# Two residual layers on one core: where SBUF tiles lie, and at which steps a fused unit prepares its second half

## The chip, the cores and the metric

The program runs on one core of a Trainium2 chip. The metric is the device time of an execution in microseconds; lower is better. A program is executed several times for its median, and once more under the hardware profiler.

## The reference

Two layers alternate, twice each, on 2048 tokens of 1024 features, all in float32 (B_* and A_* are weights):

```
x = A_q
x = x + A(layernorm(x))      # q * (long causal convolution of shifted k times v)
x = x + B(layernorm(x))      # relu(x @ w1 + b1)**2 @ w2 + b2
x = x + A(layernorm(x))
x = x + B(layernorm(x))
```

w1 is 1024 x 3584 and w2 is 3584 x 1024. The convolution runs along the tokens, per feature; its result does not depend on x, which only multiplies it.

## The kernel before

**Tiling.** Tokens are worked in four blocks of 512. Seven units are done in the order of `ORDER`; each is the dense layer B of one block (`(layer, block)`), and the convolution's products, its transforms and the layer norms are woven between its steps. A step is twelve matmuls. Every float32 operand is split into a rounded part and a rest ("hi" and "lo", type fp32r), so that one product takes three matmuls: hi by hi, hi by lo, lo by hi (`mm3`, L348 to L351). The weights' rounded part is cast on ScalarE (L1072), the rest subtracted on VectorE or GpSimd (L1080; the table `WLO` names the engines in turn, V or G, for a phase of the program). Some split weights are kept in HBM and come back as pairs (whl<-wd_m).

**Two kinds of step.** In a step of the first matrix (called m1) activations move through the array and weights stand in it: moving operand `xh` or `xl`, standing operand `whl`. In a step of the second matrix the weights move and the squared activations stand: moving `whl`, standing `rh` or `rl`, and in unit 5 also tiles named cx, cg, cp and fy (called w2 here).

**Pools.** SBUF tiles come from pools that lie one behind the other: const, pre, mw, and then cv, with a pool for the first block or ml behind it. mw holds a pad `pad_m` of 128 B, xh and xl (16 KiB each), 8 raw weight rows wr (2 KiB each) and 6 split weights whl (4 KiB each). cv begins with four tiles fx that take 2080 B each; the tiles that stand in the array in w2 steps follow at whole multiples of 256 B. When the convolution is over, cv is closed and a pool pp, the arena, opens at the place where cv began: a pad `pad_q` of 128 B, five tiles tq (16 KiB each), three sr (8 KiB), two zr (6 KiB). Each pool is laid out per partition, so these sizes give how far apart two operands are.

**The joint unit.** The last entry of `ORDER` handles two blocks at once (`make_duo`), called the joint unit, with a scheme of seven products for four. It has 196 steps in three phases: 28 steps a1 (m1 type, on the first of the two blocks), 70 steps b1 (moving tq, standing whl; five products for each of 14 pairs p), 98 steps c2 (moving whl, standing tq; seven products, each over the 14 pairs). Work beside the steps is put off by `lag.at(d, ...)`: it is written into the engines' queues d ticks later; there is one tick ahead of each step, then the weights' preparation (`w_advance`), then the step's matmuls. Each engine takes its own queue in order, so what is written at a tick stands behind all that was written earlier, and SyncE (SP) issues nearly all DMAs in that one order too.

While a1 runs, `side` prepares the second block's tokens for b1, 128 tokens (tt) at a time, in links k = 0 to 10: loads (0), mean and variance (1), gate and residual sum (2, `combine`), mean and variance again and a store (3), normalisation (4: scalars on VectorE, L1844, two passes on ScalarE, L1846), transposes on TensorE (5, L1853), differences (6 and 7), and the split into the five tq tiles (8 to 10). `SIDE_AT` gives for each tt the tick of its link 0; the links follow at fixed distances. PSUM results of a1 leave by ScalarE (L1886) and VectorE (L1900).

b1 leaves squared activations in HBM, in groups HD of four entries of 128 x 512 floats, in the order in which c2 uses them (`hd_put`, L1825). c2 loads a group with one DMA (`h_load`, L1968), rounds it on ScalarE (`h_hi`, L1972) and subtracts on VectorE (`h_lo`, L1977). Its buffers are the tq ring of five: at c2's opening, tiles that b1 still reads. c2 also reloads the residual rows of both blocks (`r_load`, L1993), adds the bias b2 to them on GpSimd (`r_bias`, L1996), adds the products from PSUM (`r_add`, L1999, VectorE) and stores.

Of the kernel before, what the change touches and what calls it, by code (L numbers as in the profile page):

```python
# [19 lines left out]
P = 128  # L20
# [47 lines left out]
WLO = {"b": "GGGV", "x": "GGGV", "b1": "VVG", "c2": "VG"}  # L68
SIDE_AT = ((2, 3), (3, 4), (0, 9), (1, 14))
# [177 lines left out]
def tile_h3_mlp(ctx: ExitStack, tc: tile.TileContext, q, kT, vT, shk, ssmT, ssmD, w1, b1, w2, b2,  # L247
# [61 lines left out]
    V.memset(pad_p, 0.0)  # L309
    b1t = const.tile([P, P], F32)  # L310
# [510 lines left out]
    def combine(x, y, m, r):  # L821
        for h in range(2):
            sl = slice(h * 512, (h + 1) * 512)
            V.scalar_tensor_tensor(y[:, sl], x[:, sl], m, y[:, sl], op0=OP.subtract, op1=OP.mult)
            V.scalar_tensor_tensor(x[:, sl], y[:, sl], r, x[:, sl], op0=OP.mult, op1=OP.add)

    def prep_w(l, b, lag):
# [4 lines left out]
        def early(tt, k):  # L832
# [5 lines left out]
            elif k == 1:  # L838
                combine(st["x"], st.pop("y"), mv[:, tt, 0:1], r[:, tt:tt + 1])
# [275 lines left out]
    pad_m = mw.tile([P, PAD_M], F32)  # L1115
    V.memset(pad_m, 0.0)
# [686 lines left out]
    def make_duo(xT):  # L1803
# [23 lines left out]
        def side(st, tt, k):  # L1827
            if k == 0:
                st["x"] = load_x(1, b2_, tt)
                st["s"] = arena[0].tile([P, 4, 512], F32, name="sr", bufs=3)  # L1830
                SY.dma_start(st["s"][:, 0:2].rearrange("p a n -> p (a n)"), YD[b2_][:, tt])
# [6 lines left out]
            elif k == 2:  # L1838
                r = rstd_b(st["ve"], st["sd"])
                combine(st["x"], st["s"][:, 0:2].rearrange("p a n -> p (a n)"), st["mv"][:, 0, 0:1], r)  # L1840
            elif k == 4:
                r = rstd_b(st["ve"], st["sd"])
                nr = pre.tile([P, 1], F32, name="nr", bufs=4)
                V.scalar_tensor_tensor(nr, st["mv"][:, 0, 0:1], -1.0, r, op0=OP.mult, op1=OP.mult)  # L1844
                for h in range(2):
# [119 lines left out]
        def h_load(g):  # L1965
            n = HD[g].shape[1]
            t = hs[g] = arena[0].tile([P, 2, DUO_G, 512], F32R, name="tq", bufs=5)
            SY.dma_start(t[:, 1, 0:n].bitcast(F32), HD[g])  # L1968

        def h_hi(g, i):  # L1970
            t = hs[g]
            A.copy(t[:, 0, i:i + 2], t[:, 1, i:i + 2].bitcast(F32))  # L1972

        def h_lo(g, i):
            t = hs[g]
            lo = t[:, 1, i:i + 2]
            V.tensor_sub(lo, lo.bitcast(F32), t[:, 0, i:i + 2].bitcast(F32))  # L1977
# [29 lines left out]
        def go(k, p, j, w, xT):  # L2007
# [3 lines left out]
            if k == "a1":  # L2011
                if s == 0:
                    lag.at(20, load_b2, bst)
# [6 lines left out]
            elif k == "b1":  # L2020
                if s == 0:
# [4 lines left out]
                    for x in range(n_p):  # L2026
                        lag.at(5 * x + 6, get_a11, x)
# [18 lines left out]
                for g, x in ((0, 8), (1, 5)):  # L2046
                    if left == x:
                        h_plan(g)
            else:
                if s == 0:  # L2050
                    for x, (e, h) in enumerate(((0, 1), (1, 0), (1, 1))):
                        lag.at(1 + x, r_load, e, h)
                        for n in range(4):
                            lag.at(5 + x + n, r_bias, e, h, n)
                    lag.at(8, r_load, 0, 0)
                    for n in range(4):
                        lag.at(11 + n // 2, r_bias, 0, 0, n)
                if s % DUO_G == 0 and s // DUO_G + 2 < len(HD):
                    h_plan(s // DUO_G + 2)
# [260 lines left out]
```

## Time and profile before

| | |
|---|---|
| Median of 3 runs | 2732.11 us (2728.47 to 2737.31) |
| The profiled execution, its own time | 2726.12 us |
| Span from first to last instruction | 2724.3 us |
| TensorE (PE) busy | 2661.5 us, 98% |
| VectorE (DVE) busy | 1997.0 us, 73% |
| ScalarE (ACT), GpSimd (POOL) busy | 1103.4 us, 1068.9 us |
| Mean granted TensorE clock | 0.994 |

A row of a profile view names the line of the kernel, the engine, the operation, the written tile and the tiles read (for a matmul the moving operand stands first, unless it is a transpose), how many there are, their busy time and the mean duration of one. A matmul's duration is longer than the distance to the next one, since they overlap. "Idle" is the time that an engine waited just before, with what released it. PEclk is the granted share of TensorE's clock. "SPq" is SyncE's queue, from which DMAs are issued.

### The profile page before, as it was taken

The page shows a single profiled execution, that of the slowest core. Times are in us where ns is not written, and L with a number is a line of the kernel's source. Part 1 is how long each engine was busy: PE and PEld are TensorE (multiplying, and loading weights), DVE is VectorE, ACT ScalarE, POOL GpSimd, SP SyncE. Part 2 cuts the span into 40 slices and gives each one's busy share as a digit, 9 for nine tenths or more (in the row PEclk, how much of TensorE's full clock was granted, in tenths as well). Part 3 has the DMA queues.
Part 4 walks back from the last instruction along what each step waited for, and adds up shares of the span by engine and source line. Part 5 has one row for each costly group of instructions (what it writes and reads, how often), then busy time and mean ns, then how long its engine had stood idle before and what let it go on. Part 6 is the DMA issues. An engine that isn't in the chain of part 4 may idle for free.

```text
span 2724.3 us, 36231 instructions
## 1 busy us (share of the span) xinstructions
PE 2661.5 (98%) x12433; PEld 2208.3 (81%) x12433; DVE 1997.0 (73%) x2926; ACT 1103.4 (41%) x1882; POOL 1068.9 (39%) x681
## 2 busy tenths in 40 slices
PE   7999999899999999999999999999999999999999
PEld 7888787788888888888888888888788778877887
DVE  7878888689887877779777666366777877766553
ACT  4454344334444333342333422345455454443432
POOL 2336565255542645327554365000100155536221
PEclk9999999999999999999999999999999999999999
DMA  8789898689989898788987878688898877768553
GB/s 262 260 303 312 284 308 284 219 289 371 340 290 316 309 335 293 271 305 304 334 278 259 315 271 290 214 292 285 298 313 274 292 269 236 239 237 310 203 191 122
DMA packets 379112, 761.32 MB, mean 279 GB/s; under 512 B 43936, under 2 KB 159280, under 8 KB 375856
## 3 DMA queue, kind: packets, MB, share of 16 engines
q1 hardware_dynamic: 378928, 759.01, 81.2%
q8 instruction: 98, 1.61, 0.2%
q14 instruction: 86, 0.70, 0.1%
HBM read 583.75 MB, written 175.11 MB: 279 GB/s over the span
## 4 chain that ended last, share of the span: by engine, by line
PE 81%; DMA 8%; DVE 6%; POOL 2%; SPq 1%; ACT 1%; issue 1%; DVEq 0%; ACTq 0%; POOLq 0%
PE p L350 24%; PE p L349 24%; PE p L351 24%; DMA wr<-w 2%; PE p L1156 2%; DMA whl<-wd_m 2%; PE pt L349 2%; PE pt L350 2%; PE pt L351 2%; DMA cg<-gd 1%; DMA hd<-xh 1%; DVE whl L1080 1%; DMA px<-x 0%; SPq L639 0%; DVE st L710 0%
## 5 line engine op out<-in xcount | busy, mean ns | idle before, releaser
L539 POOL TENSOR_TENSOR cp<-cx,cg 128x384 f32<-128x384 f32 (+5 forms) x288 | 544.2, 1903 | 582.0 <-DVE sm L543 387.7
L349 PE MATMUL p<-xh,whl 128*128 128x512 f32 (+1 forms) x1504 | 577.5, 384 | 2.4 <-DMA whl<-wd_m 2.4
L351 PE MATMUL p<-xh,whl 128*128 128x512 f32 (+1 forms) x1504 | 573.7, 381 | 0.6 <-POOL whl L1080 0.6
L350 PE MATMUL p<-xl,whl 128*128 128x512 f32 (+1 forms) x1504 | 573.2, 381 | 0.1
L1072 ACT CAST whl<-wr 128x512 fp32r<-128x512 f32 x545 | 331.5, 618 | 482.1 <-PE p L351 293.4
L349 PE MATMUL p<-whl,rh 128*128 128x512 f32 x1204 | 481.5, 400 | 3.1 <-ACT whl L1072 1.5
L350 PE MATMUL p<-whl,rh 128*128 128x512 f32 x1204 | 477.0, 396 | 4.5 <-DVE whl L1080 4.5
L351 PE MATMUL p<-whl,rl 128*128 128x512 f32 x1204 | 476.4, 396 | 0.0
L1080 DVE TENSOR_TENSOR whl<-wr,whl 128x512 fp32r<-128x512 f32 x479 | 426.7, 901 | 64.0 <-ACT whl L1072 59.1
L349 PEld LDWEIGHTS p<-xh,whl 128*128 128x128 f32 x1504 | 284.1, 189 | 56.8 <-issue 2.1
L351 PEld LDWEIGHTS p<-xh,whl 128*128 128x128 f32 x1504 | 283.4, 188 | 55.5 <-POOL whl L1080 0.8
L350 PEld LDWEIGHTS p<-xl,whl 128*128 128x128 f32 x1504 | 283.7, 189 | 52.6 <-DVE xl L1469 0.3
L1559 DVE TENSOR_TENSOR rl<-wr,rh 128x512 fp32r<-128x512 f32 x140 | 139.5, 997 | 183.6 <-ACT rh L1556 183.5
L350 PEld LDWEIGHTS p<-whl,rh 128*128 128x128 f32 x1204 | 227.9, 189 | 56.3 <-DVE whl L1080 6.2
L349 PEld LDWEIGHTS p<-whl,rh 128*128 128x128 f32 x1204 | 228.0, 189 | 55.8 <-DMA whl<-wd_m 3.0
L351 PEld LDWEIGHTS p<-whl,rl 128*128 128x128 f32 x1204 | 227.6, 189 | 53.2
L543 DVE TENSOR_REDUCE sm<-cp 128x128 f32<-128x384 f32 (+5 forms) x288 | 249.2, 873 | 10.1 <-POOL cp L539 10.1
L1551 ACT ACTIVATE wr<-p,b1t 128x512 f32<-128x512 f32 x138 | 95.2, 690 | 371.4 <-PE p L351 368.8
L1080 POOL TENSOR_TENSOR whl<-wr,whl 128x512 fp32r<-128x512 f32 x66 | 90.8, 1377 | 267.2 <-ACT whl L1072 264.7
L1679 DVE TENSOR_TENSOR acc<-p,acc 128x512 f32<-128x512 f32 x152 | 100.9, 686 | 87.0 <-PE p L351 86.6
L1977 DVE TENSOR_TENSOR tq<-tq 128x1024 fp32r<-128x1024 f32 x49 | 68.4, 1395 | 89.3 <-ACT tq L1972 89.3
L689 POOL TENSOR_TENSOR sm<-sm 128x512 f32<-128x512 f32 x48 | 68.8, 1433 | 132.9 <-DVE sm L543 125.5
(348 smaller groups left out, 4361.3 us busy)
## 6 DMA issues: line engine op xcount, KB each, us to landing
whl<-wd_m SPq DMA_DIRECT2D x323, 512.0 KB, 5.6
wr<-w SPq DMA_DIRECT2D x441, 256.0 KB, 5.4
wd_m<-whl SPq DMA_DIRECT2D x70, 512.0 KB, 6.4
wr<-td SPq DMA_DIRECT2D x112, 256.0 KB, 4.9
cx<-xd SPq DMA_DIRECT2D x48, 512.0 KB, 5.6
cg<-gd SPq DMA_DIRECT2D x48, 512.0 KB, 6.5
tq<-hd SPq DMA_DIRECT2D x24, 1024.0 KB, 6.9
gd<-fg SPq DMA_DIRECT2D x72, 256.0 KB, 6.3
```

Source lines behind the costliest of these rows:

```text
L349: PE.matmul(o, lh, rh, start=start, stop=False)
L350: PE.matmul(o, lh, rl, start=False, stop=False)
L351: PE.matmul(o, ll, rh, start=False, stop=stop)
L539: G.tensor_mul(pr.rearrange("p c i -> p i c"), xt[:, 0:j + 1], gt[:, j::-1])
L543: V.tensor_reduce(sm[:, ty, jj], st["pr"], axis=AX.X, op=OP.add)
L689: E.tensor_add(s[:, 1:3], s[:, 1:3], s[:, 0:1].to_broadcast([P, 2, s.shape[2]]))
L1072: A.copy(t[:, 0], raws[n]["t"])
L1080: ENG[e[n % len(e)]].tensor_sub(t[:, 1], raws[n]["t"], t[:, 0].bitcast(F32))
L1551: A.activation(r, st["o"], AF.Relu, bias=b1t[:, st["f"]:st["f"] + 1])
L1559: V.tensor_sub(st["lo"], st["r"]["t"], st["hi"].bitcast(F32))
L1679: V.tensor_add(accs[tt][:, d], o, accs[tt][:, d])
L1977: V.tensor_sub(lo, lo.bitcast(F32), t[:, 0, i:i + 2].bitcast(F32))
```

## The change

It has four parts.

**Places.** `pad_m` moves from mw into cv and becomes its first tile; `pad_q` is gone. So all of mw lies 128 B lower, cv's other tiles stay where they were, and the tq tiles lie 256 B lower than before.

**The links of `side`.** The distances from link 0 become (0, 3, 4, 5, 6, 9, 10, 11, 12, 13, 14) in place of (0, 2, 3, 4, 5, 6, 7, 8, 9, 10, 11), and some starts change. For the tile tt = 1 the convolution's part comes in two rows of the raw weights' ring, and its sr tile is taken only at link 4.

**Groups.** The first HD group has two entries in place of four, and is loaded into the two px tiles of pool pre, at the step with 12 of b1 left. The next three are loaded at the last three steps of b1; the later ones are loaded 10 steps ahead of their use (8 before) and split later after their load.

**c2's rest.** The bias is loaded at c2's fifth tick (it was in a1), the bias sums on GpSimd are spread over ticks 8 to 26 (5 to 12 before), the first product's sums on VectorE come six ticks later, and in c2 GpSimd subtracts one weight in three in place of one in two. `get_a11` comes four ticks earlier.

The diff, cut to its core:

```diff
-WLO = {"b": "GGGV", "x": "GGGV", "b1": "VVG", "c2": "VG"}
-SIDE_AT = ((2, 3), (3, 4), (0, 9), (1, 14))
+WLO = {"b": "GGGV", "x": "GGGV", "b1": "VVG", "c2": "VVG"}
+SIDE_AT = ((2, 2), (3, 4), (0, 9), (1, 11))
...
+    pad_m = cv.tile([P, PAD_M], F32)
+    V.memset(pad_m, 0.0)
...
-    pad_m = mw.tile([P, PAD_M], F32)
-    V.memset(pad_m, 0.0)
...
-        HD = [dram.tile([P, min(DUO_G, len(order) - g), 512], F32, name=f"hd{g}") for g in range(0, len(order), DUO_G)]
-        at = {x: (HD[n // DUO_G], n % DUO_G) for n, x in enumerate(order)}
+        group = [(0, n) if n < 2 else ((n - 2) // DUO_G + 1, (n - 2) % DUO_G) for n in range(len(order))]
+        HD = [dram.tile([P, DUO_G if g else 2, 512], F32, name=f"hd{g}") for g in range(group[-1][0] + 1)]
+        at = {x: (HD[group[n][0]], group[n][1]) for n, x in enumerate(order)}
...
-            pad_q = arena[0].tile([P, PAD_M], F32)
-            V.memset(pad_q, 0.0)
...
-                st["s"] = arena[0].tile([P, 4, 512], F32, name="sr", bufs=3)
-                SY.dma_start(st["s"][:, 0:2].rearrange("p a n -> p (a n)"), YD[b2_][:, tt])
+                if tt == 1:
+                    st["y"] = [row() for _ in range(2)]
+                    ys = [x["t"] for x in st["y"]]
+                else:
+                    st["s"] = arena[0].tile([P, 4, 512], F32, name="sr", bufs=3)
+                    ys = [st["s"][:, h] for h in range(2)]
+                for h, y in enumerate(ys):
+                    SY.dma_start(y, YD[b2_][:, tt, h * 512:(h + 1) * 512])
...
-            for k, d in enumerate((0, 2, 3, 4, 5, 6, 7, 8, 9, 10, 11)):
+            for k, d in enumerate((0, 3, 4, 5, 6, 9, 10, 11, 12, 13, 14)):
...
-            t = hs[g] = arena[0].tile([P, 2, DUO_G, 512], F32R, name="tq", bufs=5)
-            SY.dma_start(t[:, 1, 0:n].bitcast(F32), HD[g])
+            if g:
+                t = arena[0].tile([P, 2, DUO_G, 512], F32R, name="tq", bufs=5)
+                hs[g] = t[:, 0], t[:, 1]
+            else:
+                hs[g] = [pre.tile([P, 2, 512], F32R, name="px", bufs=2) for _ in range(2)]
+            SY.dma_start(hs[g][1].bitcast(F32), HD[g])
...
-        def h_plan(g):
+        def h_plan(g, first=4, gap=2):
             h_load(g)
             for i in range(0, HD[g].shape[1], 2):
-                lag.at(4 + i, h_hi, g, i)
-                lag.at(5 + i, h_lo, g, i)
+                lag.at(first + i // 2, h_hi, g, i)
+                lag.at(first + gap + i // 2, h_lo, g, i)
...
-                for g, x in ((0, 8), (1, 5)):
-                    if left == x:
-                        h_plan(g)
+                if left == 12:
+                    h_plan(0)
+                if left in (2, 1, 0):
+                    h_plan(3 - left, 3, 1)
...
-                    for x, (e, h) in enumerate(((0, 1), (1, 0), (1, 1))):
-                        lag.at(1 + x, r_load, e, h)
+                    lag.at(4, load_b2, bst)
+                    for x, (e, h) in enumerate(((0, 1), (1, 0), (1, 1), (0, 0))):
+                        lag.at((1, 2, 3, 15)[x], r_load, e, h)
                         for n in range(4):
-                            lag.at(5 + x + n, r_bias, e, h, n)
-                    lag.at(8, r_load, 0, 0)
-                    for n in range(4):
-                        lag.at(11 + n // 2, r_bias, 0, 0, n)
-                if s % DUO_G == 0 and s // DUO_G + 2 < len(HD):
-                    h_plan(s // DUO_G + 2)
+                            lag.at((8 + x + 3 * n, 20 + 2 * n)[x == 3], r_bias, e, h, n)
+                if (s + 10 - 2) % DUO_G == 0 and 4 <= (s + 8) // DUO_G + 1 < len(HD):
+                    h_plan((s + 8) // DUO_G + 1)
...
-                            lag.at(1 + n * (j in (1, 6, 7)), r_add, x // 2, x % 2, n, os[n])
+                            lag.at(1 + n * (j in (1, 6, 7)) + 6 * (j == 1), r_add, x // 2, x % 2, n, os[n])
```

Up to the joint unit the instructions stand in the same order on every engine as before, except for the pads' memsets. Inside it they move. The first place is ScalarE's queue in a1, from the normalisation of tt = 2 (the first sr<-px) to the first copy of its transposes (sr<-p). In the kernel before:

```order
L718 ACTIVATE sd<-mv_20309,epst 128x1
L1846 ACTIVATE sr<-px,nr,rs 128x512 x2
L718 ACTIVATE sd<-mv_20358,epst 128x1
L1895 ACTIVATE wr<-wr,b1t 128x512
L1896 ACTIVATE wr<-wr 128x512
L1886 COPY wr<-p_20335 128x512
L1846 ACTIVATE sr<-px,nr,rs 128x512 x2
L1860 COPY sr<-p_20396 128x512
```

The same piece of the changed kernel, whose lines are numbered some ten higher:

```order
L1856 ACTIVATE sr<-px,nr,rs 128x512 x2
L1905 ACTIVATE wr<-wr,b1t 128x512
L1906 ACTIVATE wr<-wr 128x512
L1896 COPY wr<-p_20325 128x512
L720 ACTIVATE sd<-mv_20379,epst 128x1
L1856 ACTIVATE sr<-px,nr,rs 128x512 x2
L1905 ACTIVATE wr<-wr,b1t 128x512
L1906 ACTIVATE wr<-wr 128x512
L1896 COPY wr<-p_20400 128x512
L1870 COPY sr<-p_20451 128x512
```

Between the normalisation of tt = 2 and the copy of its transposes there now stands the squaring and eviction work of two pairs of a1 (L1905 to L1896 twice), where that of one stood.

The second place is SyncE's queue at the end of b1. The tiles hd_20122, hd_20123 and hd_20124 are the first three groups; hd<-zr and the like are the stores of b1's results, wr<-w are c2's raw weights. Before, the first group's load stands eight steps ahead of c2, in the tq ring:

```order
L1922 DMA xl<-hd_20124 128x512
L1825 DMA hd_20142<-xl 128x512
L1968 DMA tq<-hd_20122 128x2048
L1825 DMA hd_20131<-xh 128x512
L1062 DMA wr<-w 128x512 x3
L1968 DMA tq<-hd_20123 128x2048
L1825 DMA hd_20128<-zr 128x512
```

In the changed kernel that load is gone to an earlier place (px<-hd_20122, behind the stores of the pair before), and the next groups stand here:

```order
L1932 DMA xl<-hd_20125 128x512
L1825 DMA hd_20132<-xh 128x512
L1065 DMA wr<-w 128x512
L1981 DMA tq<-hd_20123 128x2048
L1065 DMA wr<-w 128x512
L1981 DMA tq<-hd_20124 128x2048
L1065 DMA wr<-w 128x512
L1981 DMA tq<-hd_20125 128x2048
```

The loads into the tq ring moved behind the raw weights and the reloads of all pairs (xl<-hd is the reload `get_a11`), to b1's last three steps.

More of the change, by code (lines that the diff above doesn't have):

```diff
@@ L819, in prep_b, with combine @@
         return xh, xl
-    def combine(x, y, m, r):
-        for h in range(2):
+    def combine(x, ys, m, r):
+        for h, y in enumerate(ys):
             sl = slice(h * 512, (h + 1) * 512)
-            V.scalar_tensor_tensor(y[:, sl], x[:, sl], m, y[:, sl], op0=OP.subtract, op1=OP.mult)
-            V.scalar_tensor_tensor(x[:, sl], y[:, sl], r, x[:, sl], op0=OP.mult, op1=OP.add)
+            V.scalar_tensor_tensor(y, x[:, sl], m, y, op0=OP.subtract, op1=OP.mult)
+            V.scalar_tensor_tensor(x[:, sl], y, r, x[:, sl], op0=OP.mult, op1=OP.add)
     def prep_w(l, b, lag):
@@ L1829, in side @@
                 st["x"] = load_x(1, b2_, tt)
-                st["s"] = arena[0].tile([P, 4, 512], F32, name="sr", bufs=3)
-                SY.dma_start(st["s"][:, 0:2].rearrange("p a n -> p (a n)"), YD[b2_][:, tt])
+                if tt == 1:
[4 more added lines that the diff above has]
+                    ys = [st["s"][:, h] for h in range(2)]
+                for h, y in enumerate(ys):
+                    SY.dma_start(y, YD[b2_][:, tt, h * 512:(h + 1) * 512])
+                st["ys"] = ys
             elif k in (1, 3):
@@ L1844, in side @@
                 V.scalar_tensor_tensor(nr, st["mv"][:, 0, 0:1], -1.0, r, op0=OP.mult, op1=OP.mult)
+                if "s" not in st:
+                    st["s"] = arena[0].tile([P, 4, 512], F32, name="sr", bufs=3)
                 for h in range(2):
@@ L2063, in go @@
                 os = banks[0]
-                t = hs[s // DUO_G]
-                hi, lo = t[:, 0, s % DUO_G], t[:, 1, s % DUO_G]
+                hi, lo = (t[:, group[s][1]] for t in hs[group[s][0]])
                 for n in range(4):
```

20 lines of the change are left out of this document (9 added, 11 removed).

## The prediction, made before the changed kernel ran

> **What bounds the kernel now.** The page comes first. The first line of the fence is the span, the second the busy time of TensorE and its weight loads and of VectorE, then the matmul groups of the second matrix; the last two are ScalarE's and VectorE's share of preparing weights.
>
> ```profile
> span 2724.3 us, 36231 instructions
> PE 2661.5 (98%) x12433; PEld 2208.3 (81%) x12433; DVE 1997.0 (73%) x2926; ACT 1103.4 (41%) x1882; POOL 1068.9 (39%) x681
> L349 PE MATMUL p<-whl,rh 128*128 128x512 f32 x1204 | 481.5, 400 | 3.1 <-ACT whl L1072 1.5
> L350 PE MATMUL p<-whl,rh 128*128 128x512 f32 x1204 | 477.0, 396 | 4.5 <-DVE whl L1080 4.5
> L351 PE MATMUL p<-whl,rl 128*128 128x512 f32 x1204 | 476.4, 396 | 0.0
> L1080 DVE TENSOR_TENSOR whl<-wr,whl 128x512 fp32r<-128x512 f32 x479 | 426.7, 901 | 64.0 <-ACT whl L1072 59.1
> ```
>
> TensorE is the bound nearly everywhere, so there are two ways to shorten the program: matmuls that follow each other faster, and the few waits. Where the waits lie is told by the stretches of the span (columns: us, busy time of PE, PEld, DVE, ACT, POOL, granted clock, DMA share, GB/s). The last three are a1, b1 and c2 of the joint unit.
>
> ```profile
> 0.00:600.00 600.00, 559.40 (x2983) 482.30 (x2984) 486.41 (x742) 255.07 (x453) 275.37 (x211) 0.99 0.84 279
> 600.00:1200.00 600.00, 599.29 (x2808) 498.06 (x2807) 495.42 (x691) 235.77 (x422) 274.57 (x162) 1.00 0.90 311
> 1600.00:2146.00 546.00, 544.37 (x2417) 445.77 (x2415) 358.58 (x658) 222.96 (x374) 69.17 (x40) 1.00 0.82 278
> 2146.00:2240.00 94.00, 85.48 (x371) 70.17 (x371) 69.59 (x134) 51.24 (x94) 38.16 (x27) 0.95 0.84 298
> 2240.00:2437.00 197.00, 196.34 (x840) 157.17 (x838) 136.67 (x172) 91.34 (x146) 106.15 (x73) 1.00 0.70 232
> 2437.00:2724.30 287.30, 276.71 (x1176) 223.18 (x1175) 148.56 (x165) 106.36 (x149) 93.84 (x65) 0.99 0.62 212
> ```
>
> Outside the first 600 us, TensorE idles only in a1 (8.5 us) and at c2 (10.6). That a busy TensorE is not always equally fast shows in four stretches in which it never waits (columns: us, PE busy and matmuls, clock, DMA share, GB/s): the second matrix (w2), the first matrix (m1), b1 and c2.
>
> ```profile
> 2020.10:2058.60 38.50, 38.50 (x167) 1.00 0.81 265
> 2059.50:2102.00 42.50, 42.50 (x189) 1.00 0.93 307
> 2241.00:2431.00 190.00, 190.00 (x816) 1.00 0.69 228
> 2490.00:2719.00 229.00, 229.00 (x987) 1.00 0.55 185
> ```
>
> A stretch counts matmuls that only reach into it, so one duration (0.39 us) is added before dividing: w2 38.89/167 = 232.9 ns, m1 42.89/189 = 226.9, b1 190.39/816 = 233.3, c2 229.39/987 = 232.4. All are at clock 1.00, and m1, the fastest, runs beside the highest DMA share (0.93), so neither clock nor DMA is the reason. Nor is it the operands' roles: in b1 as in m1 activations move and weights stand, and b1 is slow. What the slow kinds share is the distance from moving to standing operand. From the pool sizes, xh and xl lie whole multiples of 512 B from whl (m1); from whl to cv's standing tiles, and between whl and tq, there remain odd multiples of 128 B (128 B over a multiple of 256).
>
> **The change part by part: places.** After it tq lies 24576 B from whl's place, a multiple of 512 B as in m1. cv's standing tiles lie 256 B over a multiple of 512, a remainder that occurs in no stretch of this trace. m1's distance stays.
>
> b1: 840 matmuls x (233.3 - 226.9) = 5.4 us. c2: 1176 x (232.4 - 226.9) = 6.5 us; group 0 (24 of them) stands in px, whose distance is another, worth 0.1 us at most. Both take the row with the same remainder, m1's; the other end is nothing, if the distance isn't the reason.
>
> w2 in the first six units: 3 x 1204 = 3612 matmuls. If a remainder of 256 is as good as 0, each saves 232.9 - 226.9 = 6.0 ns: 21.7 us. In the first 600 us TensorE is 93% busy and waits for others; part of the gain there turns into wait, so I take 20. The other end is nothing (it behaves like 128), and nothing excludes a loss, since the remainder isn't seen: each nanosecond more costs 3.6 us. I take 6 ns since the three slow kinds have in common that they are not multiples of 256 (their remainders by 512 differ: 128 in w2, 384 in b1), so 256 is the simplest period; that it is 512 is as well compatible with the rows and is a rival.
>
> **The links.** In a1 TensorE waits twice for a transpose's operand. The first fence is from the waits (us in total, times, longest), the second TensorE's order in time behind the second wait.
>
> ```profile
> PE p L1853 <- ACT sr L1846: 8.1, 2, 4.7
> ACT sr L1846 <- DVE nr L1844: 11.4, 2, 6.7
> ```
>
> ```profile
> 2196.36 1.97 PE L1853 MATMUL p<-ident,sr 128*128 128x128 f32 x8 [4.71 <-ACT sr L1846]
> 2197.98 0.78 PE L349 MATMUL p<-xh,whl 128*128 128x512 f32 x1
> 2198.55 0.63 PE L350 MATMUL p<-xl,whl 128*128 128x512 f32 x1
> 2198.98 0.63 PE L351 MATMUL p<-xh,whl 128*128 128x512 f32 x1
> ```
>
> Behind the wait matmuls come 0.43 us apart for a while (granted clock below), about double. The whole stage gives the upper bound: 336 matmuls x 0.2269 + four sets of transposes at 0.79 (an undisturbed set: 2108.14 to 2108.93) + 3 matmuls that reach in = 80.1 of 94.0 us, 13.9 over.
>
> ```profile
> 2108.14 1.04 PE L867 MATMUL p<-ident,px 128*128 128x128 f32 x8
> 2108.93 0.48 PE L349 MATMUL p<-whl,rh 128*128 128x512 f32 x1
> 2171.00:2175.50 4.50, 3.65 (x14) 0.62 1.04 320
> 2192.00:2203.00 11.00, 6.64 (x21) 0.69 0.59 188
> ```
>
> The lower bound is the waits alone, 8.1. I take 12: 8.1 and about 4 of slow matmuls. The waits belong to tt = 2 (transposes at tick 3 + 6 = 9) and tt = 0 (9 + 6 = 15). VectorE's queue holds tt = 3's gate and sum (L824, L825) ahead of tt = 2's nr, hence "ACT <- DVE nr":
>
> ```profile
> 2168.70 0.75 DVE L825 SCALAR_TENSOR_TENSOR px<-sr,rs,px 128x512 f32<-128x512 f32 x1
> 2170.79 0.16 DVE L1844 SCALAR_TENSOR_TENSOR nr<-mv,rs 128x1 f32<-128x1 f32 x1
> ```
>
>  Now the transposes come at ticks 2 + 9 = 11 and 9 + 9 = 18. A step is 12 x 0.2269 = 2.72 us: tt = 2 gets two more steps and starts one earlier (8.2 us in all, against the other wait, 8.1 - 4.7 = 3.4), tt = 0 three more steps (8.2 against the wait of 4.71). What is late next is tt = 1: its transposes stay at tick 20, its start moves from 14 to 11, and with the waits gone tick 20 comes some 10 us earlier on TensorE's clock while VectorE's work doesn't shrink (69.59 of 94 us, some 69.6 of 82). I leave 1.5 us for that: 10.5 us saved, bounds 4 (a wait as before at one transpose) to 13.9. ScalarE has one pair's evictions more ahead of tt = 2's copy; that copy only feeds b1's tiles, and the last link is still at tick 25 (11 + 14, before 14 + 11) of 28: nothing. The two rows that tt = 1 takes from the raw weights' ring leave six of eight for some ticks; the worst wait for a raw weight here is "ACT whl L1072" below, 4.3 us, and those end in ScalarE's idle time: nothing, at most 4.3.
>
> **Groups.** The waits, then TensorE's order in time at c2's opening:
>
> ```profile
> SPq L1968 <- PE p L351: 19.2, 1, 19.2
> ACT whl L1072 <- DMA wr<-w: 15.8, 5, 4.3
> PE p L350 <- DVE whl L1080: 4.9, 1, 4.9
> PE p L351 <- POOL whl L1080: 0.6, 1, 0.6
> PE p L350 <- POOL whl L1080: 1.8, 1, 1.8
> ```
>
> ```profile
> 2436.75 0.40 PE L349 MATMUL p<-whl,tq 128*128 128x512 f32 x1
> 2442.03 0.80 PE L350 MATMUL p<-whl,tq 128*128 128x512 f32 x1 [4.88 <-DVE whl L1080]
> 2448.09 0.39 PE L349 MATMUL p<-whl,tq 128*128 128x512 f32 x1
> ```
>
> SyncE stands 19.2 us at group 0's load, because the ring's tile is still read by b1; behind it are the reload xl<-hd and c2's raw weights. VectorE then sits in order before the last difference of b1 and only after it makes the weight's rest:
>
> ```profile
> 2440.08 0.69 DVE L1960 TENSOR_TENSOR zr<-zr,xl 128x512 f32<-128x512 f32 x1 [5.15 <-DMA xl<-hd]
> 2441.29 0.68 DVE L1080 TENSOR_TENSOR whl<-wr,whl 128x512 fp32r<-128x512 f32 x1
> ```
>
> From 2436.75 to 2448.09 are 16 matmuls in 11.34 us; at 0.227 they take 3.6. So 7.7 us, with b1's 0.6 ahead 8.3. Group 0 now needs no ring tile and comes 12 steps (33 us) ahead; the ring loads come at b1's last three steps, when of the five tiles the first, second and third have had their last step (tile 6 is done four steps before the end). Behind them on SyncE stand raw weights, and if a load waited they would be late again, at the same 8.3 us. A group's landing takes 5.1 to 10.1 us:
>
> ```profile
> DMA to landing us min/median/max: 5.1/6.9/10.1
> ```
>
> Group 1 is split three ticks after its load (8.2 us) and used five steps after it (13.6). Rounding and subtraction of two entries are about 1.2 us each (VectorE's mean is 1395 ns on the page), so even 10.1 + 2.6 = 12.7 is in time. I take 8.3; the other end is 0.
>
> **c2's rest.** The 1.8 us wait for GpSimd comes behind four bias sums in its queue, which end at 2487.7:
>
> ```profile
> 2481.24 6.46 POOL L1996 TENSOR_TENSOR xh<-xh,px 128x512 f32<-128x512 f32 x4
> ```
>
> Spread out, and with a third instead of half of the weights, GpSimd has the time: 1.8 saved. VectorE takes the others at 0.9 us each; it is busy 148.56 of 287.30 us, so that hides. If it didn't, one late weight costs what the 4.9 us row does.
>
> **Sum.** 5.4 + 6.5 + 20 + 10.5 + 8.3 + 1.8 = 52.5 us off the profiled execution's 2726.1: 2673.6. The median of the runs stands 6.0 above that execution, so 2679.6, rounded 2680. Its own range, with the waits' bounds (up to 12 less saved, or up to 3.4 more in a1 and 1.7 more in w2, and the runs' own spread of some 9 us), is 2666 to 2692.
>
> **The rivals.** (1) *256 is like 128*: w2 saves nothing, 2679.6 + 20 = 2699.6. For it: only multiples of 512 are seen fast. Against: 384 and 128 behave alike.
>
> (2) *The distance counts for nothing*, and m1 is faster for another reason: only the waits go, 20.6 us, 2711.5. For it: three kinds differ from m1 in more than distance. Against: b1 has m1's roles and b1 is slow. The Trainium skill ("TensorE: Matmul & The Clock Gate", section "Step-by-step: what each phase is for") states a rule on this side: the moving operand and the next weight load have separate read ports of SBUF, and the load takes no read bandwidth from the running matmul. By that rule no address could matter; the trace, with 226.9 against 232.9 ns at one clock, speaks against it.
>
> (3) *256 is worse than 128*, in the 3612 matmuls of w2; this is the one that ends slower. Everything else gains 32.5, so the gain is gone from 32.5/3612 = 9.0 ns more, a pitch of 241.9, and the kernel is slower by over 0.3% (8.2 us) from 11.3 ns more, 244.2. At 250 ns it would be 2699.6 + 17.1 x 3.612 = 2761. For it: nothing in the trace shows the remainder. Against: no undisturbed stretch is above 233.3.
>
> (4) *The waits move, they don't go*: VectorE's queue is late at tt = 1 instead, and SyncE waits at a ring load: 10.5 + 8.3 + 1.8 stay, 2679.6 + 20.6 = 2700. For it: VectorE's work in a1 is the same in less time. Against: the slack worked out above.
>
> **How the numbers follow.** 0.3% of the time, 8.2 us, is about what a measurement of this kernel can tell from no change. Chances: forecast 0.52, (1) 0.18, (2) 0.07, (3) 0.15, (4) 0.08. Of (3) a third each is still faster, the same, and slower. So faster 0.90, same 0.05, slower 0.05. The range 2666 to 2712 takes in the forecast's own range, (1), (4) and most of (2); what is left out is (3) and the forecast's edges, some 0.2.
>
> **What would show it.** In the changed profile: undisturbed stretches of w2, b1 and c2 at 226.9 ns each (w2 at 232.9 means rival 1, above it rival 3; b1 and c2 unchanged means rival 2); a1 beginning some 20 us earlier, at about 2126; no wait of TensorE at the transposes over 1.5 us and a clock near 1.00 in a1; no wait of SyncE at the group loads, and c2's first 16 matmuls in under 4 us. A median above 2712, or a w2 pitch above 233, makes the prediction wrong.

## The result, and the profile after

The changed kernel takes 2691.33 us (median of 4 runs, 2687.2 to 2693.22) against 2733.44 us (median of 4, 2728.47 to 2737.31): a ratio of 0.9845, 95% interval 0.9825 to 0.9865. The forecast was 2680, its range 2666 to 2712. The profiled execution took 2691.26 us, 34.9 less than that of before; 52.5 less were forecast.

The page of the changed kernel, the lines that answer to the first fence of the prediction; its lines are numbered one to ten higher (L349 to L351 are L351 to L353 now):

```profile
span 2689.5 us, 36226 instructions
PE 2631.0 (98%) x12433; PEld 2207.3 (82%) x12433; DVE 2003.0 (74%) x2942; ACT 1106.0 (41%) x1882; POOL 1045.9 (39%) x664
```

As many matmuls keep TensorE busy for 30.5 us less, so they follow each other faster. The stretches of the changed kernel's span, cut where the first matmul of a stage starts (us, busy time of PE, PEld, DVE, ACT, POOL, clock, DMA share, GB/s): a1, b1 and c2.

```profile
2131.10:2227.30 96.20, 87.44 (x369) 70.31 (x370) 74.42 (x131) 52.04 (x94) 38.63 (x26) 0.93 0.77 279
2227.30:2417.70 190.40, 190.40 (x842) 157.66 (x841) 138.88 (x181) 94.27 (x151) 109.04 (x74) 1.00 0.82 260
2417.70:2689.50 271.80, 266.88 (x1177) 220.52 (x1175) 154.44 (x173) 104.37 (x144) 71.21 (x47) 1.00 0.62 213
```

The same cuts in the kernel before:

```profile
2146.40:2239.60 93.20, 85.02 (x369) 69.81 (x370) 69.02 (x132) 51.24 (x94) 37.76 (x27) 0.95 0.84 297
2239.60:2436.75 197.15, 196.49 (x841) 157.52 (x840) 136.84 (x172) 91.09 (x146) 106.55 (x73) 1.00 0.70 232
2436.75:2724.30 287.55, 276.96 (x1177) 223.18 (x1175) 148.56 (x165) 106.61 (x149) 93.84 (x65) 0.99 0.62 212
```

So a1 begins 15.3 us earlier, is 3.0 longer, b1 is 6.75 and c2 15.75 shorter: 34.8 in all. In b1 TensorE never waits: 840 matmuls in 190.4 us, 226.7 ns each. The first and the last matmul of an undisturbed stretch of w2 in the changed kernel, 122 matmuls apart:

```profile
1868.85 0.39 PE L353 MATMUL p<-whl,rl 128*128 128x512 f32 x1
...
1896.50 0.39 PE L352 MATMUL p<-whl,cx 128*128 128x512 f32 x1
```

27.65 us over 122 are 226.6 ns. The same 122 matmuls before took 28.34 us, 232.3 ns each:

```profile
1883.56 0.39 PE L351 MATMUL p<-whl,rl 128*128 128x512 f32 x1
...
1911.90 0.39 PE L350 MATMUL p<-whl,cx 128*128 128x512 f32 x1
```

At c2's opening, in the changed kernel:

```profile
2417.68 0.40 PE L351 MATMUL p<-whl,px 128*128 128x512 f32 x1
...
2423.28 0.39 PE L351 MATMUL p<-whl,tq 128*128 128x512 f32 x1
```

The 24 matmuls of group 0 in px take 5.60 us without a wait, where 16 took 11.34. That they are 233.3 ns apart again fits the place of px, 64 B over a multiple of 256 B from whl. What went wrong is a1. TensorE's waits there in the changed kernel:

```profile
PE p L1863 <- ACT sr L1870: 2.7, 1, 2.7
PE p L351 <- DMA whl<-wd_m: 2.4, 2, 1.8
PE p L351 <- DVE wr L1910: 1.9, 1, 1.9
PE p L1863 <- DVE sr L1872: 1.6, 2, 0.8
PE p L351 <- ACT wr L1896: 0.7, 1, 0.7
```

No transpose waits for its operand any more (L1856, the former L1846, is gone from the list), but the waits' sum is 9.3 us (0.6 of it at a1's very first matmul), against 8.5 before (8.1 at the transposes, 0.4 at the first matmul). For 6.9 us of it PSUM is waited for: transposes wait until the copy and the subtractions of link 6 (L1870, L1872) have read earlier transposes, and m1's matmuls until pairs are evicted (L1896, L1910). A wait of 1.8 us is of another kind: it is for a weight pair, issued at 2165.71 us, that took 8.2 us to land. The slow clock came along, in three stretches (us, PE busy, clock, DMA share, GB/s):

```profile
2174.30:2177.70 3.40, 3.40 (x9) 0.50 0.80 272
2187.90:2191.30 3.40, 3.40 (x10) 0.51 0.51 165
2198.20:2205.00 6.80, 5.96 (x18) 0.50 0.84 282
```

They are 13.6 us at about half the clock; before, the prediction's two rows (0.62 over 4.5 us, 0.69 over 11) come to 10.2 us at half of it. So 0.8 us more of waits and 1.7 us more for the clock are 2.5 of the 3.0 us that a1 lost.

That the readers of PSUM come late shows in VectorE's busy time in three stretches of a1 in the changed kernel (us, VectorE busy, clock, DMA share, GB/s):

```profile
2131.00:2150.00 19.00, 11.18 (x24) 1.00 0.98 383
2150.00:2164.00 14.00, 8.20 (x27) 1.00 0.87 285
2164.00:2205.00 41.00, 36.15 (x65) 0.83 0.71 253
```

It is 59% busy up to 2164 us and 88% in the 41 us in which all of the waits but one of 0.6 us lie. The share alone proves little: in the same 41 us it is 90% in e3 and 86% in e9 below, whose waits differ. And just ahead of these 41 us VectorE stands still:

```profile
2164.16 0.69 DVE L1910 TENSOR_TENSOR wr<-p,wr 128x512 f32<-128x512 f32 x1 [5.37 <-DMA hd<-wr]
```

It waits for a row of the raw weights' ring that a store still reads. SyncE issued that store at 2157.89, after it had stood until 2155.67 for VectorE's own residual sum; it took 6.1 us to land. The kernel before has no such wait, and the two rows that tt = 1 takes from this ring are new. The theory from here on: **places** set the matmuls' spacing; **groups and c2's rest** did what was forecast; **the links** only moved a1's waits, since VectorE has too much to do, in order, in these ticks.

### The profile page after: what moved, and what is told of

It is laid out like the page before. It is cut to its first block, busy times and chain, and to the rows that moved or that the text cites. A ratio compares the mean times of both kernels' runs of the same rounds, so it can differ in the third digit from the quotient of the medians.

```text
span 2689.5 us, 36226 instructions
## 1 busy us (share of the span) xinstructions
PE 2631.0 (98%) x12433; PEld 2207.3 (82%) x12433; DVE 2003.0 (74%) x2942; ACT 1106.0 (41%) x1882; POOL 1045.9 (39%) x664
## 4 chain that ended last, share of the span: by engine, by line
PE 82%; DVE 7%; DMA 6%; issue 2%; ACT 2%; SPq 1%; POOL 1%; DVEq 0%; ACTq 0%; POOLq 0%
PE p L352 24%; PE p L353 24%; PE p L351 24%; PE p L1157 2%; PE pt L352 2%; PE pt L353 2%; PE pt L351 2%; DMA wr<-w 1%; DVE whl L1083 1%; DMA cg<-gd 1%; DMA wd_m<-whl 1%; DMA whl<-wd_m 1%; DVE sm L545 0%; PE p L805 0%; SPq L641 0%
## 5 line engine op out<-in xcount | busy, mean ns | idle before, releaser
L351 PE MATMUL p<-xh,whl 128*128 128x512 f32 (+1 forms) x1504 | 578.7, 385 | 8.2 <-DMA whl<-wd_m 5.5
L353 PE MATMUL p<-xh,whl 128*128 128x512 f32 (+1 forms) x1504 | 574.2, 382 | 0.6 <-POOL whl L1083 0.6
L351 PE MATMUL p<-whl,rh 128*128 128x512 f32 x1204 | 475.4, 395 | 1.7 <-DMA whl<-wd_m 1.0
L352 PE MATMUL p<-whl,rh 128*128 128x512 f32 x1204 | 470.9, 391 | 5.1 <-DVE whl L1083 4.9
L353 PE MATMUL p<-whl,rl 128*128 128x512 f32 x1204 | 470.4, 391 | 0.0
L351 PEld LDWEIGHTS p<-xh,whl 128*128 128x128 f32 x1504 | 284.6, 189 | 63.7 <-ACT rh L1616 2.6
L353 PEld LDWEIGHTS p<-xh,whl 128*128 128x128 f32 x1504 | 284.2, 189 | 55.6 <-POOL whl L1083 0.8
L351 PEld LDWEIGHTS p<-whl,rh 128*128 128x128 f32 x1204 | 227.3, 189 | 49.1 <-DMA whl<-wd_m 2.3
L353 PEld LDWEIGHTS p<-whl,rl 128*128 128x128 f32 x1204 | 226.9, 188 | 47.7
L1083 POOL TENSOR_TENSOR whl<-wr,whl 128x512 fp32r<-128x512 f32 x49 | 71.5, 1459 | 267.0 <-ACT whl L1075 245.3
L351 PE MATMUL p<-tq,whl 128*128 128x512 f32 x280 | 108.9, 389 | 0.0
```

What stands on the lines that cost most here:

```text
L351: PE.matmul(o, lh, rh, start=start, stop=False)
L352: PE.matmul(o, lh, rl, start=False, stop=False)
L353: PE.matmul(o, ll, rh, start=False, stop=stop)
L1083: ENG[e[n % len(e)]].tensor_sub(t[:, 1], raws[n]["t"], t[:, 0].bitcast(F32))
```

## The experiments

The kernel before, run beside each group, had medians of 2730.86 us (e1 to e4), 2728.28 (e5 to e8), 2730.29 (e9 to e11) and 2729.38 (e12); a ratio compares with those. For w2, stretches run over the same 122 matmuls.

**e1, the places alone** (the kernel before, with):

```diff
+    pad_m = cv.tile([P, PAD_M], F32)
+    V.memset(pad_m, 0.0)
...
-    pad_m = mw.tile([P, PAD_M], F32)
-    V.memset(pad_m, 0.0)
...
-            pad_q = arena[0].tile([P, PAD_M], F32)
-            V.memset(pad_q, 0.0)
```

> The kernel before with the change's places alone (the pad in cv, no second pad); no instruction moves. Theory (distance): what the changed kernel gained in matmul spacing is all due to the places, so w2 saves the 15.3 us by which a1 began earlier there, b1 840 x 6.5 ns = 5.5 and c2 1176 x 5.7 ns = 6.7, and the waits of a1 and of c2's opening stay: 2733.4 - 27.5 = 2706, with undisturbed stretches of w2, b1 and c2 at 226.7 ns. Rival (order): b1 and c2 run faster because of the new order of their loads, not of the places: only 15.3 us saved, 2718, b1 still at 233 ns.

Measured: 2702.46 us, ratio 0.9895 (0.987 to 0.992), 28.4 less than before. Its a1, b1 and c2:

```profile
2132.50:2226.03 93.53, 84.24 (x368) 68.72 (x369) 69.13 (x130) 51.37 (x94) 38.65 (x27) 0.96 0.83 295
2226.03:2417.86 191.83, 190.99 (x841) 157.55 (x840) 134.69 (x172) 90.87 (x146) 105.43 (x73) 1.00 0.71 238
2417.86:2700.20 282.34, 270.40 (x1177) 222.00 (x1175) 149.11 (x165) 107.27 (x149) 94.44 (x65) 0.98 0.63 216
```

No instruction of these stages moved, and w2, b1 and c2 have 226.7 ns. The rival on the order falls. a1 (93.53) and c2's waits stay.

**e2, the order alone** (the changed kernel, with the pads as they were):

```diff
-    pad_m = cv.tile([P, PAD_M], F32)
+    pad_m = mw.tile([P, PAD_M], F32)
...
+            pad_q = arena[0].tile([P, PAD_M], F32)
```

> The changed kernel with both pads put back where they were, so the change's order of steps alone. Theory (distance): spacing as before the change (232 to 233 ns), a1 begins where it did, the gain is that of c2's opening and of its bias sums (8.3 + 1.8) less what a1 lost (3.0): 2733.4 - 7.1 = 2726. Rival (order): b1 and c2 keep 226.7 ns: 2726 - 12.2 = 2714. Rival (a1 suffers only because the matmuls before it are faster): a1 gains the predicted 10.5 and the time is 2713, with b1 at 233 ns.

Measured: 2719.42 us, ratio 0.9958 (0.9945 to 0.997), 11.4 less than before, 4 more than the theory's.

```profile
2149.91:2245.45 95.54, 86.37 (x369) 69.77 (x369) 74.22 (x131) 51.86 (x94) 39.20 (x26) 0.95 0.76 275
2245.45:2441.44 195.99, 195.99 (x841) 157.68 (x840) 140.29 (x181) 94.15 (x151) 108.76 (x74) 1.00 0.81 256
2441.44:2718.50 277.06, 273.36 (x1177) 221.36 (x1175) 152.61 (x173) 104.03 (x144) 71.44 (x47) 1.00 0.60 208
```

b1 is at 195.99/840 = 233.3 ns without any wait, and a1 is 95.5 us: the links lose 2.3 with the old spacing too, so a1 doesn't suffer from the faster matmuls ahead of it. c2 gains 287.55 - 277.06 = 10.5 and b1 1.2 (the wait at its end). With a1's loss that is 9.4; the other 2 us of the 11.4 lie within the runs' spread.

**e3, the old links** (the changed kernel, with):

```diff
-SIDE_AT = ((2, 2), (3, 4), (0, 9), (1, 11))
+SIDE_AT = ((2, 3), (3, 4), (0, 9), (1, 14))
...
-                if tt == 1:
+                if tt == NT:
...
-            for k, d in enumerate((0, 3, 4, 5, 6, 9, 10, 11, 12, 13, 14)):
+            for k, d in enumerate((0, 2, 3, 4, 5, 6, 7, 8, 9, 10, 11)):
```

> The changed kernel with the links' distances and starts as before the change (and no rows of the weights' ring for tt = 1); places, groups and the rest of c2 stay changed. Theory (the links gained nothing): a1 lasts as long as before the change, 93.2 us instead of 96.2: 2691.3 - 3 = 2688, with the two waits at the transposes back. Rival (the links hide part of what the faster weights would cost): a1 gets longer than 96.2 us, time 2692 to 2700.

Measured: 2687.88 us, ratio 0.9844 (0.9823 to 0.9864). a1, and its waits:

```profile
2132.64:2225.96 93.32, 83.78 (x369) 68.69 (x369) 71.95 (x131) 51.51 (x94) 39.01 (x27) 0.96 0.81 291
```

```profile
PE p L1863 <- ACT sr L1856: 9.5, 3, 4.7
```

As the theory has it: 93.3 us, with the waits for the operand back. VectorE's wait for the ring is gone; tt = 1 takes no rows here. Against the changed kernel the profile shows 2.9 us less in a1; in the whole time the intervals overlap.

**e4, a pad of 64 B** (the changed kernel, with):

```diff
-PAD_C, PAD_P, PAD_M = 104, 56, 32
+PAD_C, PAD_P, PAD_M = 104, 56, 16
```

> The changed kernel with a pad of 64 B in place of 128 B, so that cv's standing tiles lie 192 B over a multiple of 256 B from the moving ones; the joint unit's distances stay. Theory 1 (a multiple of 256 or not is all that counts): w2 falls back to 232.9 ns, a1 begins 15.3 us later, 2691.3 + 15.3 = 2707. Theory 2 (64 B over is worse than 128 B over, as the 24 matmuls of group 0 in px, 64 B over, hint at 233.4 ns or more): w2 at 234 to 236 ns, 2710 to 2720. Rival (distance counts for nothing): 2691.

Measured: 2696.67 us, ratio 0.9877 (0.9856 to 0.9899). First and last of the 122 matmuls of w2:

```profile
1878.49 0.39 PE L353 MATMUL p<-whl,rl 128*128 128x512 f32 x1
...
1906.41 0.39 PE L352 MATMUL p<-whl,cx 128*128 128x512 f32 x1
```

228.9 ns: neither 226.7 nor 232.9, and not worse than 128 B over. The distance counts, a1 begins 9.8 us later (2140.90), but both theories on its form fell. It is the distance and not one tile's own place: e1 moved whl and left cv's standing tiles, e4 moves these and leaves whl, and w2 changes in both; in m1, where both operands came to lie 128 B lower, 192 matmuls have 226.7 ns before (from 2059.02 us) and after (from 2044.23 us).

**e7 and e8, other distances** (the changed kernel, with the lines of e7; e8 has 36 and 24 for 56 and 8):

```diff
-PAD_C, PAD_P, PAD_M = 104, 56, 32
+PAD_C, PAD_P, PAD_M = 104, 56, 56
...
+            pad_q = arena[0].tile([P, 8], F32)
+            V.memset(pad_q, 0.0)
```

> The changed kernel with other pads: cv's standing tiles lie 96 B over a multiple of 256 B from the moving ones (w2), tq 32 B over in c2 and, with the roles exchanged, 224 B over in b1. So far stand 226.7 ns at 0, 233.3 at 64, 232.4 at 128, 229.1 at 192. Theory (a straight fall from just above 0 to 256): 96 gives 232.8, 32 gives 233.5 to 234, 224 gives 228. Rival (steps of 64 B): 96 as 64, 32 as 0, 224 as 192: 233.3, 226.7, 229.1.

> The same with tiles 32 B over a multiple of 256 B in w2, 96 B over in c2 and 160 B over in b1. Theory (straight fall): 233.5 to 234, 232.8, 230.8 ns; the kind of step does not matter, so w2 here equals c2 of the other pads and the reverse. Rival (steps of 64 B): 226.7, 233.3, 232.4.

Measured: 2723.71 and 2725.23 us (one run each). The pad of 36 floats counts as 160 B, since a tile takes whole multiples of 32 B (so an fx of 515 floats takes 2080). In w2 of e7 the 122 matmuls go from 1887.77 to 1916.36 us: 28.59 us, 234.3 ns each. All distances together, each from the first and the last start of an undisturbed stretch (122 matmuls of w2, 720 of b1, 1140 of c2; 24 for px):

| bytes over a multiple of 256 | ns from matmul to matmul (where) |
|---|---|
| 0 | 226.7 (w2, b1, c2 of the changed kernel; remainders by 512 of 256, 0 and 0) |
| 32 | 233.3 (w2 of e8, remainder by 512 of 288), 233.3 (c2 of e7, 32) |
| 64 | 233.3 (px) |
| 96 | 234.3 (w2 of e7, 352), 234.3 (c2 of e8, 96) |
| 128 | 232.3 (w2 before), 232.4 (c2 of e2), 233.3 (b1 before, roles exchanged) |
| 160 | 233.3 (b1 of e8) |
| 192 | 228.9 (w2 of e4), 229.6 (px in e2) |
| 224 | 233.3 (b1 of e7) |

The period is 256: equal remainders by 256 give equal spacing where those by 512 differ, in w2 and in c2. Within it the form is neither a straight fall nor steps of 64 B; every distance that was tried and isn't a multiple of 256 costs 2.2 to 7.6 ns. The rows mix two kinds of step: b1, where weights stand, has 233.3 ns at 128, 160 and 224 alike, and w2, c2 and px, where weights move, rise to 234.3 at 96 and fall to 229 at 192. Only 0 and 128 were tried in both kinds. Why the distance counts no run here shows; the weight loads of b1 are recorded as equally long at both spacings (PEld 157.52 us for 840 before, 157.66 for 841 after).

**e5, other ticks** (the changed kernel, with the first two tiles one tick later):

```diff
-SIDE_AT = ((2, 2), (3, 4), (0, 9), (1, 11))
+SIDE_AT = ((2, 3), (3, 5), (0, 9), (1, 11))
```

> The changed kernel with the first two tiles of the links one tick later (starts 3, 5, 9, 11), so that the reads of the transposes' PSUM (link 6) come at odd ticks, where no first_h addition stands in VectorE's queue, while it stands at the even ones. Theory (place in the queue): TensorE's waits at the transposes for these reads (0.7 + 0.8 + 2.7 us in the changed kernel) go, with the slow clock behind the last: a1 falls from 96.2 us to about 90, time 2691.3 - 6 = 2685. Rival (VectorE has too much to do between the fifth and the twentieth tick, wherever it stands): the waits come back at other places, a1 stays at 95 us or more, 2690 to 2693.

Measured: 2697.21 us, ratio 0.9886 (0.9869 to 0.9902); a1 is 102.6 us. Its waits:

```profile
PE p L351 <- DVE wr L1910: 4.5, 1, 4.5
PE p L351 <- DMA whl<-wd_m: 3.5, 3, 2.8
PE p L1863 <- ACT sr L1870: 3.4, 2, 3.0
PE p L1863 <- ACT sr L1856: 3.3, 1, 3.3
```

The theory of the place in the queue fell. With the same work in one tick less, all kinds of wait are there at once, those for the operand too.

**e6, less GpSimd beside VectorE** (the changed kernel, with):

```diff
-                        (G if j in (6, 4) else V).tensor_sub(lo, v, hi.bitcast(F32))
+                        V.tensor_sub(lo, v, hi.bitcast(F32))
```

In the changed kernel, three of VectorE's rows, and then GpSimd's that runs at the same time as the last two:

```profile
2187.44 1.28 DVE L1886 TENSOR_TENSOR tq<-sr,tq 128x512 fp32r<-128x512 f32 x2
2195.19 3.43 DVE L1886 TENSOR_TENSOR tq<-sr,tq 128x512 fp32r<-128x512 f32 x2
2199.14 0.67 DVE L1872 TENSOR_TENSOR sr<-sr,p 128x512 f32<-128x512 f32 x1
```

```profile
2196.36 3.38 POOL L1866 TENSOR_TENSOR zr<-xh,xl 128x512 f32<-128x512 f32 x2
```

Two subtractions take 3.43 us beside GpSimd and 1.28 otherwise, but L1872, which has one operand in PSUM, takes its 0.67 beside the same GpSimd operations. The Trainium skill ("SBUF — State Buffer", section "Who interferes with whom") states such a rule: a VectorE operation with two inputs in SBUF and a GpSimd operation that reads SBUF exclude each other, one with a single input in SBUF doesn't contend. The trace agrees, with these three numbers.

> The changed kernel with all five subtractions of the last link on VectorE (two were on GpSimd). Theory (stretching: VectorE's operations take two to three times as long while GpSimd works, 3.43 us for two at 2195.19 where 1.28 is usual, and that makes it late): the three subtractions take 2.0 us again and the two added ones 1.3, against 5.2 now, so TensorE's last waits shrink by some 2 us and a1 falls to 93 to 94, time 2688 to 2689. Rival (VectorE's amount of work): two more operations a tile make it later by 1.3 us, a1 97 to 98, time 2692 to 2693.

Measured: 2690.31 us, ratio 0.986 (0.9845 to 0.9874). a1 and b1:

```profile
2133.47:2225.59 92.12, 83.17 (x369) 67.30 (x369) 70.95 (x139) 50.77 (x93) 24.94 (x18) 0.98 0.77 280
2225.59:2420.44 194.85, 192.35 (x842) 158.80 (x840) 139.47 (x181) 94.81 (x153) 107.31 (x74) 0.99 0.82 259
```

VectorE does eight operations more in a1 and is busy for 70.95 us, 3.5 less: the stretching is real, and a1 is 4.1 us shorter. But b1 is 4.4 longer: at its opening a weight is late. GpSimd waits for the load of which it makes that weight, and SyncE issues the load (L1031) only behind a store of a1's squares and one of its sums:

```profile
POOL sr L1039 <- DMA sr<-w: 10.7, 1, 10.7
```

```profile
2222.28 0.32 SPq L1900 DMA_DIRECT2D hd<-wr  x1
...
2223.18 0.90 SPq L1031 DMA_DIRECT2D sr<-w  x2
```

In all, nothing is gained that the runs could tell.

**e10, the same with the old links** (e3's and e6's diffs together).

> The changed kernel with the links' distances and starts as before the change, and all five subtractions of the last link on VectorE. In a1 the waits with these links are for nr (VectorE's queue at ticks 9, 15, 20), and only the third of them stands behind such subtractions. Theory (GpSimd's operations stretch VectorE's): a1 falls from 93.3 us by 1 to 3, b1's opening waits by as much or less, time 2685 to 2688. Rival (amount of VectorE's work): later by 1.3 us a tile, a1 94 to 97, 2689 to 2692.

Measured: 2690.2 us, ratio 0.9858 (0.9842 to 0.9875); a1 93.65 us, e3's 93.3. Neither theory shows: with the old links the waits come ahead of such subtractions, and nothing changes by more than the runs differ.

**e11, the last tile later** (the changed kernel, with):

```diff
-SIDE_AT = ((2, 2), (3, 4), (0, 9), (1, 11))
+SIDE_AT = ((2, 2), (3, 4), (0, 9), (1, 13))
```

> The changed kernel with the last tile of the links two ticks later (start 13 for 11), so that VectorE's work of tt = 0 and tt = 1 lies less on top of each other. Theory (bunching of VectorE's work): the waits of 1.9, 0.7, 2.7 and 0.8 us after the third transposes shrink by half or more, with the slow clock behind them: a1 90 to 93 us, time 2685 to 2688. Rival (what counts is the end: the last split is now two ticks later, at the 27th of 28): b1's opening waits for the tiles by as much as a1 gains, 2691 or more.

Measured: 2692.82 us, ratio 0.9861 (0.9846 to 0.9876). a1 and b1:

```profile
2132.30:2225.70 93.40, 84.51 (x369) 67.75 (x369) 68.34 (x127) 45.74 (x83) 33.01 (x24) 0.96 0.78 280
2225.70:2419.88 194.18, 190.99 (x841) 157.55 (x840) 145.76 (x186) 100.69 (x162) 114.17 (x77) 1.00 0.81 260
```

a1 gains 2.8, b1 loses 3.8. The rival holds: some of the work now lies in b1's opening. VectorE's wait for the ring is gone here too, with tt = 1's rows taken two ticks later, so part of the 2.8 us may be due to that.

**e9, VectorE's work taken away** (the changed kernel, without):

```diff
-                combine(st["x"], st["ys"], st["mv"][:, 0, 0:1], r)
```

> The changed kernel without the gate and residual sum of link 2 (16 operations of 0.75 us on VectorE in a1 are left out; the second block's tokens then go on without the convolution's part). Theory (VectorE has too much to do between 2164 and 2205 us, where it is 88% busy, and everything late is late through its queue): with 12 us less the waits of TensorE mostly go, a1 falls from 96.2 us to 80 to 87. Rival (the loads of weight pairs, or the links' places, make the waits): a1 stays at 92 us or more.

Measured: 2679.04 us (one run). a1 and its waits:

```profile
2130.40:2215.84 85.44, 81.98 (x368) 67.58 (x369) 62.00 (x114) 52.02 (x94) 38.53 (x26) 0.98 0.83 307
```

```profile
PE p L1862 <- ACT sr L1869: 2.3, 1, 2.3
PE p L351 <- DMA whl<-wd_m: 1.5, 2, 1.2
PE p L1862 <- DVE sr L1871: 1.2, 1, 1.2
```

a1 falls by 10.8 us for 12 us of VectorE's work, with the same loads and the same links: m1's matmuls no longer wait for evictions. This is what the links' part did not touch. VectorE still waits 4.6 us for the ring here, so that wait alone doesn't make a1 long; what it adds beside the work was not tried by itself.

**e12, less of VectorE's work in these ticks, with nothing left out.** In the changed kernel VectorE waits 5.08 us at a1's start for the first pair:

```profile
2136.91 0.69 DVE L1910 TENSOR_TENSOR wr<-p,wr 128x512 f32<-128x512 f32 x1 [5.08 <-PE p L353]
```

And unit 5 has just summed the rows whose mean and variance link 1 computes again:

```diff
+        def first_stats():
+            mv = first["mv"] = pre.tile([P, NT, 2], F32, name="mv", bufs=2)
+            for tt in range(NT):
+                s = pre.tile([P, 2, 6], F32, name="st", bufs=2)
+                for h in range(2):
+                    V.bn_stats(s[:, h], wacc[(1, 2, 3, 6)[2 * (tt // 2) + h]][tt % 2])
+                V.bn_aggr(mv[:, tt], s)
+            first["ve"], first["sd"] = rstd_a(mv)
...
-                r = rstd_b(st["ve"], st["sd"])
-                combine(st["x"], st["ys"], st["mv"][:, 0, 0:1], r)
+                combine(st["x"], st["ys"], first["mv"][:, tt, 0:1], first["r"][:, tt:tt + 1])
...
+        lag.at(1, first_stats)
+        lag.at(2, first_r)
```

> The changed kernel with the first mean and variance of the second block's four tiles taken at a1's first tick from the rows that unit 5 has just summed in SBUF (once for all four), in place of link 1 on the reloaded rows: about 10 us of VectorE's work leave the ticks 5 to 16, 6.6 us of it are done instead where VectorE waits 5 us for the first pair of a1. Nothing is left out. Theory (VectorE's work in these ticks is what makes a1's waits): a1 falls from 96.2 us to 86 to 90, of which b1's opening may take back 2 to 4, time 2682 to 2686. Rival (work at a1's start delays the first evictions as much): a1 94 or more, 2690 or more.

Measured: 2686.08 us (median of 5, 2684.2 to 2688.09), ratio 0.9838 (0.9825 to 0.9851). a1 and b1:

```profile
2133.97:2224.81 90.84, 83.62 (x369) 68.26 (x369) 75.19 (x117) 51.22 (x91) 43.09 (x28) 0.96 0.81 297
2224.81:2415.31 190.50, 190.50 (x841) 157.58 (x840) 139.33 (x181) 94.05 (x151) 109.87 (x74) 1.00 0.83 261
```

a1 is 5.4 us shorter (a little less than the 6 to 10 of the theory), though VectorE still waits 6.1 us for the ring, and b1 gives nothing back. It is the shortest of the kernels that do all of the work, though its interval overlaps with those of e3 and of the changed kernel. Some 11 us above the 79.4 of undisturbed matmuls and transposes remain in a1.

## Why the prediction was right, and where it was not

The time lies in the range and the sign is right; of 52.5 us forecast for the profiled execution 34.9 came. (The medians differ by 42.1, because the profiled execution of before was 7.3 below its median and that of the changed kernel at its own.) By its terms:

- *b1's spacing*, forecast 5.4; *c2's*, 6.5; *c2's opening with b1's wait*, 8.3; *bias sums*, 1.8: 22.0 together. b1 and c2 gained 6.75 + 15.75 = 22.5. Apart: e2 to the changed kernel, places only, b1 195.99 to 190.40 = 5.6, c2 277.06 to 271.80 = 5.3 (6.5 up to its last matmul; what comes behind it took 1.2 longer); before to e2, order only, 1.2 + 10.5. Right in mechanism and size. One detail: SyncE waits at the ring loads after all, 4.2 us in three waits; the slack covers it.
- *w2's spacing*, forecast 20, measured 15.3 (13.9 in e1). That 256 is as good as 0 was the guess on which the sum hung most, and it held: rivals 1, 2 and 3 fall with 226.6 ns. The rule of the Trainium skill ("TensorE: Matmul & The Clock Gate", section "Step-by-step: what each phase is for") that was weighed there says that the next weight load takes no read bandwidth from the running matmul. The prediction took from it that no address could matter, and that is not so here: e1 moved nothing but addresses, and w2, b1 and c2 changed; whether the loads' reads are the cause no run shows. The sum counted 3612 matmuls and left out the 336 of unit 5 whose standing operand is cx, cg, cp or fy; 3948 at 5.7 ns would be 22.4 us, so the size is off by more than the 4.7 us. It is off at both ends of the program, where TensorE waits for others. Up to the 2765th matmul (556 us), 672 matmuls of w2 gained 1.0 us for some 4. In the last 263 us ahead of a1, 588 of them gained 0.6 for 3.4; here the waits for weight pairs have grown. All of them from 1600 us to a1, in the kernel before and then in the changed one:

```profile
PE p L349 <- DMA whl<-wd_m: 1.4, 2, 0.8
```

```profile
PE p L351 <- DMA whl<-wd_m: 3.1, 2, 2.2
```

  They grew by 1.7 of the 2.8 us that are missing there. I allowed for the first 600 us alone. What makes these pairs come late was not tried by itself.
- *a1*, forecast 10.5 saved, measured 3.0 lost: this is the step that failed. It said that later transposes give VectorE the time, and that only tt = 1 is late next, by 1.5 us. The wait for nr did go. But VectorE's queue was not late because of nr's place; it had 36 us of work in 41 us, stretched by GpSimd, and in the same queue stand the reads that free PSUM. So TensorE was stopped by PSUM instead: rival 4 in a1, though not at c2. e9 shows the cause (a1 85.4 with 12 us of work away), e12 that moving work into VectorE's idle time shortens a1 without a loss in b1, where moving the links' ticks (e5, e11) doesn't. A second term was wrong too: the two rows from the raw weights' ring were put at nothing, since only the wait for a raw weight was looked at. VectorE stands 5.4 us for that ring ahead of these 41 us, and doesn't in e3, which takes no rows, nor in e11, which takes them two ticks later. How much of a1's loss that wait makes stays open: no run has the new links without the two rows.

The miss adds up: 13.5 in a1 and 4.7 in w2, less 0.5 gained beyond the forecast in b1 and c2, are 17.7 of the 17.6 us.

## What to carry to other kernels

Where matmuls follow each other without a wait and still differ in spacing, look at how far apart their operands lie: here multiples of 256 B between moving and standing operand gave 226.7 ns against 228.9 to 234.3, for the price of one pad's place. Before a wait on an in-order engine is cured by a later consumer, add up what that engine does in those ticks and what else stands in its queue: if it is full, the wait goes to the next resource that it frees. A ring's rows taken for another use are a cost to look up as well: here an engine stood 5.4 us for one. Work is better moved to where the engine idles, and the stage behind has to be read as well (e6 and e11 gave all of a1's gain back at b1's opening).

## What of the hardware was not expected

- The spacing of matmuls has a period of 256 B in the operands' distance: 226.7 ns at its multiples; elsewhere 233.3 ns in b1 wherever it was tried, and 228.9 to 234.3 ns where weights move.
- Waits of 1.82 and 1.95 us were followed by 3.4 us at a clock of 0.50 in the changed kernel; a wait of 2.23 us in the changed kernel (up to 1922.31 us) and, before, one of 1.8 us in c2 (up to 2488.99 us) were not.
